# A fused attention and two-layer feed-forward kernel: V of one window pair and the scores of the next as one group in the same two PSUM banks, and pooled attention by two head pairs on the four corners of the array

## The chip, the cores and the metric

The kernel runs on one core of one Trainium2 chip. The metric is the device time of one execution in microseconds. The core has a matrix engine (TensorE, PE in the profile), a vector engine (VectorE, DVE), a scalar engine (ScalarE, ACT), a general engine (GpSimd, POOL) and SyncE (SP), which issues all DMAs of this kernel on one queue. PEld is the loading of weights into the array of TensorE. Every engine works through its own queue in order.

## The reference

`q`, `k`, `v` have the shape (4, 8, 576, 64): batch, heads, positions, head width. Two attentions are added, and the sum runs through two feed-forward layers.

```python
q_d, k_d, v_d = mean of 4 neighbouring positions each        # 144 positions
out_d = softmax(scale * q_d @ k_d.T) @ v_d                   # pooled attention
out_up = np.repeat(out_d, 4, axis=2)
mask = np.abs(pos[:, None] - pos[None, :]) < 4
out_local = softmax(where(mask, scale * q @ k.T, -1e9)) @ v  # band of 7 positions
x = out_up + out_local                                       # as 2304 tokens x 512
x = square(relu(x @ w_in1)) @ w_out1                         # layer one, 512 -> 2048 -> 512
h = x @ w_in2
out = (h * cos(h)) @ w_out2                                  # layer two
```

## The kernel before

The 2304 tokens are cut into 40 windows (10 per batch) of 56 to 60 queries against 64 keys for the band attention. Two neighbouring windows are a pair; there are 20 pairs. Five blocks of four pairs (460 or 464 tokens) go through layer one; layer two follows in nine blocks of 256 tokens.

Layer one is 80 units (5 blocks of 16). A unit has 12 matmuls of stage A (`stage_a`, L801, into the one bank `ps_h`) and 12 of stage B (`stage_b1`, L884, into the four banks `acc`), in a split of each fp32 number into two rounded parts (xh and xl, gh and gl, hi and lo). These 24 are called main matmuls below. Between A and B of a unit, ScalarE makes relu (L825), square (L826) and the high part (L813), and VectorE the low part (L819).

The attention of blocks one to four, and the conversion of the weights (`conv1`, `conv2`), run as tasks beside the units: Python generators that issue a step each time `advance` is called, in the order of `RANK`, from start slots set at the end of the program (`start_at`). The first block's attention runs alone, ahead of all units, in the "early" phase. A scheduler then orders the instructions of each engine by a simulated time line, so attention matmuls end up in groups between main matmuls.

A pair (`pair`, `soft`) on TensorE is: for the first blocks, the mask as a small bf16 matmul (L545); 16 score matmuls of 64 x 64 (L564), each in one corner of the 128 x 128 array (`svs[a][halves_of[c], ...]`: row half a, column half c), into two banks; after the softmax two transposes (L503) per half; and 16 V matmuls (L606), again in corners, into two banks `avs` that are asked for anew. VectorE adds the pooled part (L623), ScalarE and VectorE write xh and xl (L635, L637). PSUM has three banks `ps_a` for all of this.

The pooled attention of a batch is `pool` (loads and sums over four positions, L368, L373, L375; L371 copies the two halves of q into a zero-padded tile `qp`, so that one matmul covers two heads) and four tasks `down`, one for each head pair: three score matmuls with 96 columns of weights over 128 rows (L412), softmax, six transposes of 96 rows (L433), four V matmuls of 64 columns and 72 rows (L449).

The matmuls of `pair` and `down` have plain fp32 operands; each of them is two records in the trace. The transposes and the main matmuls are one record each.

Of the kernel before, what the change touches and what calls it, by code (L numbers as in the profile page):

```python
# [8 lines left out]
F32 = mybir.dt.float32  # L9
# [9 lines left out]
P = 128  # L19
# [11 lines left out]
QROWS = 2 * SD // 3  # L31
DM = H * D
# [16 lines left out]
PE_POOLED = 0  # L49
# [15 lines left out]
RANK = {"down": 0, "pair": 1, "pool": 2, "conv1": 3, "conv2": 3}  # L65
# [27 lines left out]
def kernel(  # L93
# [37 lines left out]
    for t, v in zip(magic, (MAGIC, -MAGIC)):  # L131
# [10 lines left out]
        "a": 3, "h": 1, "acc": 4, "qkw": 2, "vw": 2, "pr": 4, "pt": 5, "xt": 2, "qp": 1, "xd": 2, "vp": 1, "av": 3, "pl": 2, "raw": 2,  # L142
        "dpr": 2, "dpt": 1, "qk0": 0,
# [36 lines left out]
    kept = [spare.pop() for _ in range(W0[1] // 4 + 1)]  # L180
# [28 lines left out]
    lent = {"pr": ["pr"] * caps["pr"] + ['gt', 'gt', 'gl', 'gl'], "pt": ["pt"] * caps["pt"] + ['gh', 'gh', 'gh']}  # L209

    def band_tile(name, shape):
# [5 lines left out]
        if tag == name:  # L217
            return tag, cm.tile(shape, F32, tag=name, name=name, bufs=caps[name])
        t = gp.tile([P, TMAX], F32R if tag in ("gh", "gl") else F32, tag=tag, name=name, bufs=3 if tag == "gh" else 2)
        n = shape[1] * shape[2]  # L220
        return tag, t.bitcast(F32)[:shape[0], :n].rearrange("p (a b) -> p a b", a=shape[1])

    def band_done(name, tag):
        if early[0]:
            lent[name].append(tag)
# [18 lines left out]
    qp = cm.tile([P, HPAIR, 2, SD], F32, name="qp", bufs=1)  # L244
    for a in range(2):
        nc.gpsimd.memset(qp[(1 - a) * D:(2 - a) * D, :, a], 0.0)
    def pool(b):
# [8 lines left out]
        for i, hp in parts:  # L256
# [20 lines left out]
            if b < PE_POOLED:  # L277
                if not early[0]:
                    yield
                bank, = yield from need_a()  # L280
                pe_pool(bank, loaded, kp, vp)
                done_a(bank)
                done("pl")
                done("pl")
                loaded = []
# [48 lines left out]
    def pe_pool(bank, pieces, kp, vp):  # L334
        c0 = 0
        for i, hp, t in pieces:
            if isinstance(i, int):
                rows, cols = P, SD
                tv = t.rearrange("p (j r) -> p r j", r=FACTOR)
            else:  # L340
                rows, cols = KTOK, len(i) * P
                tv = t.rearrange("p (c r) -> p r c", r=FACTOR)
            o = bank[:rows, c0:c0 + cols]
            c0 += cols
            for r in range(FACTOR):
                last["pe"] = nc.tensor.matmul(
                    o, ident[:rows, :rows], tv[:, r], start=r == 0, stop=r == FACTOR - 1
                ).ins
            if i == 0:
                for a in range(2):  # L350
                    half = slice(a * D, (a + 1) * D)
                    nc.scalar.copy(out=qp[half, hp, a], in_=o[half])
            elif i == 1:
                nc.vector.tensor_copy(out=kp[:, hp], in_=o)
            else:
                nc.vector.tensor_copy(
                    out=vp[:, i[0]:i[-1] + 1, hp * P:(hp + 1) * P], in_=o.rearrange("p (k c) -> p k c", k=len(i))
                )

# [4 lines left out]
    def pool_piece(i, hp, t, kp, vp):  # L364
        tv = t.rearrange("p (j r) -> p j r", r=FACTOR)
        if i == 0:
            qc = cm.tile([P, SD], F32, tag="qc", name="qc", bufs=1)
# [33 lines left out]
    def down(b, hp):  # L401
# [8 lines left out]
        qf = qp[:, hp].rearrange("p a s -> p (a s)")  # L410
        for m in range(3):
            last["pe"] = nc.tensor.matmul(sv[:, m], qf[:, m * QROWS:(m + 1) * QROWS], kp[:, hp], start=True, stop=True).ins  # L412
# [5 lines left out]
        yield from exps(s, sv, mx, pr, SCALE / FACTOR ** 2, b < 2)  # L418
# [8 lines left out]
        if not early[0]:  # L427
            yield
# [853 lines left out]
```

## Time and profile before

| what | value |
|---|---|
| median of three runs | 916.42 us (915.8 to 916.44) |
| the profiled execution's own time | 915.9 us |
| its span, first to last instruction | 914.1 us |
| TensorE busy | 891.4 us (98%) |
| VectorE busy | 645.6 us (71%) |
| ScalarE busy | 573.0 us (63%) |
| mean granted TensorE clock | 0.990 of full speed |

The span is what the views of the trace cover; 1.8 us of the execution lie around it. Layer one's first main matmul starts at about 43 us, layer two's first at about 517 us, among the last of layer one. A busy TensorE in such a table is not a TensorE at its peak: how far two starts lie apart tells more than how long one matmul lasts.

### The profile page before, as it was taken

To read this page: it belongs to the slowest core of one execution; us is meant where nothing else is said; L and a number is where in the kernel's file an instruction comes from. 1 tells how busy PE (TensorE), PEld (TensorE's weight loads), DVE (VectorE), ACT (ScalarE), POOL (GpSimd) and SP (SyncE) were. 2 spreads that over 40 slices of the span, in tenths; PEclk is the share of its full clock that TensorE was granted. 3 is DMA by queue.
4 is the path that set the end of the run, shared out by engine and by line. 5 is a ranking of instruction groups with operands and counts; after the bars stand their busy time and mean duration, and the time that the engine had idled before them with its cause. 6 is when DMAs were issued, how large, how long until landed. Compare 5 with 4: busy or idle time off the path is not lost.

```text
span 914.1 us, 17776 instructions
## 1 busy us (share of the span) xinstructions
PE 891.4 (98%) x6946; PEld 814.0 (89%) x6946; DVE 645.6 (71%) x1266; ACT 573.0 (63%) x1039; POOL 97.7 (11%) x79
## 2 busy tenths in 40 slices
PE   7799999999999999999999999999999999999997
PEld 5577788888887888889998999999999999999997
DVE  6999897555766657563311188888888887888786
ACT  5677785455645555454534477776777677777774
POOL 2001320122303313221200000000000000000000
PEclk9799999999999999999999999999999999999999
DMA  9588888867898766884897966655666656566663
GB/s 279 185 324 306 285 305 286 285 254 256 300 331 282 266 231 213 310 307 172 287 386 239 355 222 204 203 187 191 203 202 200 200 200 196 190 196 205 209 227 104
DMA packets 72903, 223.55 MB, mean 245 GB/s; under 512 B 9620, under 2 KB 14612, under 8 KB 68724
## 3 DMA queue, kind: packets, MB, share of 16 engines
q1 hardware_dynamic: 72820, 222.43, 71.5%
q8 instruction: 54, 0.88, 0.4%
q14 instruction: 29, 0.24, 0.1%
HBM read 181.50 MB, written 40.89 MB: 243 GB/s over the span
## 4 chain that ended last, share of the span: by engine, by line
PE 84%; DMA 9%; DVE 3%; ACT 2%; SPq 1%; issue 1%; POOL 0%; DVEq 0%; ACTq 0%; POOLq 0%
PE ps_h L836 22%; PE acc L908 19%; PE ps_h L801 19%; PE acc L884 18%; DMA pl<-in_pool_qk_dram 3%; DMA pl<-in_pool_v_dram 3%; DMA raw<-in_w_dram 2%; DMA pv<-in_pool_v_dram 1%; PE ps_a L412 1%; PE ps_a L606 1%; PE ps_a L564 1%; PE ps_a L449 1%; PE acc L906 1%; PE ps_a L503 1%; PE ps_a L433 1%
## 5 line engine op out<-in xcount | busy, mean ns | idle before, releaser
L836 PE MATMUL ps_h<-x,w2hi 128*128 128x256 f32 x1152 | 160.1, 281 | 0.0
L819 DVE TENSOR_TENSOR gl<-gt,gh 128x460 fp32r<-128x460 f32 (+1 forms) x80 | 59.0, 738 | 141.1 <-ACT gh L813 79.5
L836 PEld LDWEIGHTS ps_h<-x,w2hi 128*128 128x128 f32 x1152 | 146.9, 188 | 0.1
L908 PE MATMUL acc<-bl,gh 128*128 128x256 f32 x504 | 140.6, 280 | 0.0
L801 PE MATMUL ps_h<-xh,w1hi 128*128 128x460 f32 (+1 forms) x320 | 123.3, 386 | 7.4 <-ACT gt L825 3.7
L884 PE MATMUL acc<-gl,w1hi 128*128 128x460 f32 (+1 forms) x320 | 120.5, 377 | 0.2 <-DVE gl L819 0.2
L801 PE MATMUL ps_h<-xl,w1hi 128*128 128x460 f32 (+1 forms) x320 | 120.5, 377 | 0.0
L825 ACT ACTIVATE gt<-ps_h 128x460 f32<-128x460 f32 (+1 forms) x80 | 44.2, 554 | 104.3 <-PE ps_h L801 104.1
L884 PE MATMUL acc<-gh,w1hi 128*128 128x460 f32 (+1 forms) x320 | 107.2, 376 | 0.0
L884 PE MATMUL acc<-gh,lo 128*128 128x460 f32 (+1 forms) x256 | 95.3, 372 | 0.0
L908 PEld LDWEIGHTS acc<-bl,gh 128*128 128x128 f32 x504 | 94.8, 188 | 0.0
L876 DVE TENSOR_TENSOR gl<-g,gh 128x896 fp32r<-128x896 f32 x72 | 78.2, 1087 | 11.0 <-ACT gh L871 11.0
L844 ACT ACTIVATE u<-ps_h,quarter 128x512 f32<-128x512 f32 x72 | 49.4, 687 | 52.6 <-PE ps_h L836 52.4
L908 PE MATMUL acc<-w2hi,gh 128*128 128x256 f32 x288 | 80.7, 280 | 0.0
L908 PE MATMUL acc<-w2hi,gl 128*128 128x256 f32 x288 | 80.2, 280 | 0.0
L851 DVE SCALAR_TENSOR_TENSOR r<-u,ps_h 128x512 f32<-128x512 f32 x72 | 49.4, 687 | 41.3 <-ACT u L846 40.5
L801 PEld LDWEIGHTS ps_h<-xh,w1hi 128*128 128x128 f32 x320 | 60.7, 190 | 17.1 <-ACT gt L825 5.1
L871 ACT ACTIVATE gh<-g 128x896 fp32r<-128x896 f32 x72 | 68.1, 945 | 10.2 <-DVE g L869 10.2
L856 ACT ACTIVATE r<-r,half_pi 128x512 f32<-128x512 f32 x72 | 51.8, 720 | 34.7 <-DVE r L852 34.7
L836 PE MATMUL ps_h<-x,w2lo 128*128 128x256 f32 x432 | 68.5, 280 | 0.0
L884 PEld LDWEIGHTS acc<-gl,w1hi 128*128 128x128 f32 x320 | 60.1, 188 | 7.6 <-DVE gl L819 1.2
L801 PEld LDWEIGHTS ps_h<-xl,w1hi 128*128 128x128 f32 x320 | 60.8, 190 | 6.2
(147 smaller groups left out, 1903.0 us busy)
## 6 DMA issues: line engine op xcount, KB each, us to landing
bl<-wo_d SPq DMA_DIRECT2D x70, 896.0 KB
raw<-in_w_dram SPq DMA_DIRECT2D x32, 1024.0 KB
lo<-lo_d SPq DMA_DIRECT2D x128, 256.0 KB
qkw<-in_win_qk_dram SPq DMA_DIRECT2D x16, 512.0 KB
pl<-in_pool_qk_dram SPq DMA_DIRECT2D x24, 288.0 KB
wo_d<-raw SPq DMA_DIRECT2D x16, 384.0 KB
out_dram<-o SPq DMA_DIRECT2D x18, 256.0 KB
vw<-in_win_v_dram SPq DMA_DIRECT2D x16, 256.0 KB
```

The costliest lines, as they stand in the source:

```text
L412: last["pe"] = nc.tensor.matmul(sv[:, m], qf[:, m * QROWS:(m + 1) * QROWS], kp[:, hp], start=True, stop=True).ins
L801: nc.tensor.matmul(h[:, :n], a[:, c * P:(c + 1) * P], x[:, c, :n], start=i == 0, stop=i == len(order) - 1)
L819: last["gl"] = nc.vector.tensor_tensor(out=gl, in0=gt, in1=gh.bitcast(F32), op=ALU.subtract).ins
L825: last["relu"] = nc.scalar.activation(out=gt, in_=h, func=AF.Relu).ins
L836: nc.tensor.matmul(h[:, s * TB:(s + 1) * TB], a[:, c * P:(c + 1) * P], x[:, c], start=i == 0, stop=i == len(order) - 1,)
L844: nc.scalar.activation(out=u, in_=h, func=AF.Identity, bias=quarter, scale=float(1.0 / (2 * math.pi)))
L851: nc.vector.scalar_tensor_tensor(out=r, in0=u, scalar=-PI2_HI, in1=hv, op0=ALU.mult, op1=ALU.add)
L856: nc.scalar.activation(out=r, in_=r, func=AF.Sin, bias=half_pi, scale=1.0)
L871: nc.scalar.activation(out=gh, in_=g[:, 1:], func=AF.Copy)
L876: nc.vector.tensor_tensor(out=gl, in0=g[:, 1:], in1=gh.bitcast(F32), op=ALU.subtract)
L884: nc.tensor.matmul(acc[d][:, :n], a, x, start=f == 0 and i == 0, stop=f == NF - 1 and i == 2)
L908: nc.tensor.matmul(o, a[:, x], b, start=opens and i == 0, stop=p == NP2 - 1 and i == 2 and (k % 2 == 1 or k == NPROD - 1),)
```

## The change

- `down` serves batch 0 alone. For batches 1 to 3 a task `down_two` serves two head pairs at once. Its scores are 12 matmuls of 64 x 64 weights over 144 columns, one head each, in the four corners (row half a: head of the pair; column half c: head pair). The queries are taken in three parts of 48; the weights have 64 columns, so 16 rows of each part hold what is not used. The transposes are then of 128 rows in place of 96. The V matmuls stay, eight in one go.
- `qp` needs no zero padding for these, so the sum over positions writes q directly, without the copies L371. The tile is lengthened by a strip of zeros.
- In `pair`, the score matmuls are now a function. When V of a pair is issued and the next pair waits with its scores, these are issued right behind, into the upper halves of the same two banks (V uses 256 columns of 512). A pair waits for that unless it is `alone`; V is held back a little for a next pair that is about to come (`held_for_next`).
- One buffer fewer for `pt`, one more for `dpt`; the unused `pe_pool` is gone.

```diff
-RANK = {"down": 0, "pair": 1, "pool": 2, "conv1": 3, "conv2": 3}
+RANK = {"down": 0, "down_two": 0, "pair": 1, "pool": 2, "conv1": 3, "conv2": 3}
...
-        "a": 3, "h": 1, "acc": 4, "qkw": 2, "vw": 2, "pr": 4, "pt": 5, "xt": 2, "qp": 1, "xd": 2, "vp": 1, "av": 3, "pl": 2, "raw": 2,
-        "dpr": 2, "dpt": 1, "qk0": 0,
+        "a": 3, "h": 1, "acc": 4, "qkw": 2, "vw": 2, "pr": 4, "pt": 4, "xt": 2, "qp": 1, "xd": 2, "vp": 1, "av": 3, "pl": 2, "raw": 2,
+        "dpr": 2, "dpt": 2, "qk0": 0,
...
-            if t is not None:
+            if t is not None and shares.pop(id(t), 1) == 1:
                 used[kinds.pop(id(t))[0]] -= 1
...
-        if i == 0:
-            qc = cm.tile([P, SD], F32, tag="qc", name="qc", bufs=1)
+        if i == 0 and not early[0]:
+            nc.vector.tensor_reduce(out=qp[:, hp, 0], in_=tv, op=ALU.add, axis=AX.X)
+        elif i == 0:
+            qc = cm.tile([P, HPAIR * 2 * WQ], F32, tag="xt", name="qc", bufs=caps["xt"])[:, :SD]
...
+    def down_soft(b, a, s, sv, pr, pts):
...
+        for kt in range(2):
+            for m in range(3):
+                last["pe"] = nc.tensor.transpose(
+                    tps[kt][:KTOK, m * P:(m + 1) * P], pr[:, m, kt * KTOK:(kt + 1) * KTOK], ident,
+                ).ins
...
+    def down_two(b, h2):
...
+        ss = yield from need_a(2)
+        svs = [s[:, :3 * SD].rearrange("r (m s) -> r m s", m=3) for s in ss]
+        halves_of = [slice(a * D, (a + 1) * D) for a in range(2)]
+        for m in range(3):
+            for c in range(2):
+                q0 = 2 * (2 * h2 + c) * SD + m * QPART
+                for a in (1, 0):
+                    rows = halves_of[a]
+                    with in_turn(m + c > 0 or a == 0):
+                        last["pe"] = nc.tensor.matmul(
+                            svs[a][halves_of[c], m], qf[rows, q0:q0 + D], kp[rows, 2 * h2 + c], start=True, stop=True,
+                        ).ins
...
+    def alone(q):
+        if q - 1 < W0[1] // 2 or placed[0] >= q or q - 1 not in scored_pairs:
+            return True
+        b = window_of(2 * q - 2)[0]
+        return any((b, hp) not in downs for hp in range(HPAIR))
+
+    def held_for_next(q, j):
+        if q + 1 == NW // 2 or q + 1 in scored_pairs or q + 1 in at_scores:
+            return False
+        return now[0] < NF * j - 3 and begins[q + 1] < now[0] + 5
...
+        if ss is None:
+            ss = yield from need_a(2)
+            svs = [s[:, :HPAIR * WK].rearrange("p (h s) -> p h s", h=HPAIR) for s in ss]
+            scores(svs)
+        else:
+            svs = [s[:, 4 * WQ:].rearrange("p (h s) -> p h s", h=HPAIR) for s in ss]
...
+        while not apart and held_for_next(q, j):
+            yield
         avs = yield from need_a(2)
...
+        if q + 1 in at_scores and q + 1 not in handed:
+            at_scores[q + 1](
+                [t[:, 4 * WQ:].rearrange("p (h s) -> p h s", h=HPAIR) for t in avs], follows=True
+            )
+            handed[q + 1] = avs
+            for t in avs:
+                shares[id(t)] = 2
...
-        for hp in range(HPAIR):
-            start_at(at + 4 + hp, down, b, hp)
+        for h2 in range(HPAIR // 2):
+            start_at(at + 4 + 2 * h2, down_two, b, h2)
```

What this does to the queue of TensorE is shown at two places. Line numbers of the change are its own: L890 and L973 are the main matmuls of stages A and B, L632 the scores and L691 the V matmuls of a pair, L484 and L453 scores and transposes of `down_two`, L559 the transposes of a pair.

TensorE before, in block four's attention (units 50 and 51): the V matmuls of pair 17 and one score matmul of pair 18 stand together, and the other 15 scores after 26 further main matmuls.

```order
L884 MATMUL acc_4560<-gh,lo 128x460
L606 MATMUL ps_a<-pt,vw 64x56 x14
L564 MATMUL ps_a<-qkw 64x64
L801 MATMUL ps_h_4603<-xh,w1hi_800 128x460
L801 MATMUL ps_h_4603<-xl,w1hi_800 128x460
```

The rest of these scores, with main matmuls on both sides:

```order
L884 MATMUL acc_4557<-gh,lo 128x460
L884 MATMUL acc_4558<-gh,w1hi_685 128x460
L564 MATMUL ps_a<-qkw 64x64 x15
L801 MATMUL ps_h_4643<-xh,w1hi_805 128x460
L801 MATMUL ps_h_4643<-xl,w1hi_805 128x460
```

TensorE with the change, the same V matmuls, now in unit 52:

```order
L973 MATMUL acc_4519<-gl,w1hi_795 128x460
L973 MATMUL acc_4519<-gh,lo 128x460
L691 MATMUL ps_a<-pt,vw 64x56 x16
L632 MATMUL ps_a<-qkw 64x64 x16
L890 MATMUL ps_h_4686<-xh,w1hi_910 128x460
L890 MATMUL ps_h_4686<-xl,w1hi_910 128x460
```

V and scores are one group of 32 matmuls where they were three groups. Eight of the 16 pairs behind the early phase are joined so.

TensorE before, pooled scores of batch 3 (unit 42): three matmuls for one head pair, then transposes of a window pair and pooled V.

```order
L884 MATMUL acc_3455<-gl,w1hi_1289 128x464
L884 MATMUL acc_3455<-gh,lo 128x464
L412 MATMUL ps_a<-kp,qp 96x144 x3
L503 MATMUL ps_a<-const_sb,pr 128x128 x2
L449 MATMUL ps_a<-dpt,vp 64x144 x4
L801 MATMUL ps_h_4085<-xh,w1hi_1524 128x464
```

TensorE with the change, pooled scores of batch 3 (unit 42): twelve matmuls for two head pairs.

```order
L973 MATMUL acc_3410<-gh,lo 128x464
L973 MATMUL acc_3411<-gh,w1hi_1271 128x464
L484 MATMUL ps_a<-kp,qp 64x144 x12
L559 MATMUL ps_a<-const_sb,pr 128x128 x2
L890 MATMUL ps_h_4062<-xh,w1hi_1515 128x464
L890 MATMUL ps_h_4062<-xl,w1hi_1515 128x464
```

Six such groups of twelve take the place of twelve groups of three; in four of the six the first matmul stands by itself, some main matmuls ahead of the other eleven.

ScalarE before, from the high part of unit 36 to the relu of unit 37 (gt, L825): an exponential (L397) stands ahead of the relu.

```order
L813 ACTIVATE gh<-gt 128x464
L684 ACTIVATE shi<-bits 128x1024
L397 ACTIVATE pr<-pr 128x256
L825 ACTIVATE gt<-ps_h_3544 128x464
L771 ACTIVATE raw<-raw 128x768
L397 ACTIVATE pr<-pr 128x256
```

ScalarE with the change, the same stretch (L914 is the relu, L915 the square, L902 the high part, L727 xh, L370 the exponential):

```order
L902 ACTIVATE gh<-gt 128x464
L773 ACTIVATE shi<-bits 128x1024
L727 ACTIVATE xh<-xt 128x4x116
L914 ACTIVATE gt<-ps_h_3492 128x464
L860 ACTIVATE raw<-raw 128x768
L915 ACTIVATE gt<-gt 128x464
L370 ACTIVATE pr<-pr 128x256
```

What stands ahead of this relu is now a copy of the sum of both attentions (xh), and the exponentials come later.

## Rows read from the trace of the kernel before

**Rows 1.** The page, busy time of the engines, and the chain that ended last.
```profile
PE 891.4 (98%) x6946; PEld 814.0 (89%) x6946; DVE 645.6 (71%) x1266; ACT 573.0 (63%) x1039; POOL 97.7 (11%) x79
...
PE 84%; DMA 9%; DVE 3%; ACT 2%; SPq 1%; issue 1%; POOL 0%; DVEq 0%; ACTq 0%; POOLq 0%
```

**Rows 2.** Busy time by stretch: length, engines (instructions), granted clock, DMA share, GB/s.
```profile
75.00:100.00 25.00, 23.24 (x153) 19.83 (x152) 22.99 (x47) 18.51 (x52) 3.74 (x3) 0.93 0.84 294
125.00:150.00 25.00, 25.00 (x214) 20.93 (x213) 21.91 (x45) 17.81 (x35) 1.64 (x2) 1.00 0.88 287
275.00:300.00 25.00, 23.00 (x167) 19.11 (x166) 15.26 (x33) 13.62 (x23) 8.07 (x5) 1.00 0.88 292
550.00:914.00 364.00, 359.11 (x3012) 357.57 (x3011) 302.95 (x561) 257.34 (x363) 0.00 (x0) 1.00 0.59 195
```

**Rows 3.** Waits of TensorE, whole span: us in total, times, longest.
```profile
PE ps_h L801 <- ACT gt L825: 3.7, 3, 2.0
...
PE ps_h L801 <- ACT w1hi L684: 1.8, 1, 1.8
PE ps_a L503 <- POOL pr L491: 1.4, 1, 1.4
```

**Rows 4.** Time line of TensorE, V matmuls: start, duration, engine, line, tile, records.
```profile
234.41 0.37 PE L884 MATMUL acc<-gh,w1hi 128*128 128x460 f32 x1
234.71 0.33 PE L606 MATMUL ps_a<-pt,vw 64*64 64x60 f32 x4
...
235.28 0.37 PE L884 MATMUL acc<-gh,lo 128*128 128x460 f32 x1
235.58 0.69 PE L606 MATMUL ps_a<-pt,vw 64*64 64x60 f32 x32
...
236.52 0.38 PE L801 MATMUL ps_h<-xl,w1hi 128*128 128x460 f32 x1
```

**Rows 5.** Time line of TensorE, pooled scores of one head pair alone.
```profile
193.73 0.37 PE L884 MATMUL acc<-gh,lo 128*128 128x460 f32 x1
193.93 0.90 PE L412 MATMUL ps_a<-kp,qp 128*96 128x144 f32 x6
194.57 0.47 PE L801 MATMUL ps_h<-xh,w1hi 128*128 128x460 f32 x1
194.88 0.38 PE L801 MATMUL ps_h<-xl,w1hi 128*128 128x460 f32 x1
195.09 0.37 PE L801 MATMUL ps_h<-xh,w1hi 128*128 128x460 f32 x1
```

**Rows 6.** Time line of TensorE, pooled transposes ahead of pooled scores.
```profile
211.19 0.66 PE L433 MATMUL ps_a<-const_sb,dpr 96*72 96x96 f32 x6
211.69 0.90 PE L412 MATMUL ps_a<-kp,qp 128*96 128x144 f32 x6
```

**Rows 7.** Time line of TensorE, scores of a pair and pooled V in one group.
```profile
228.85 0.69 PE L564 MATMUL ps_a<-qkw 64*64 64x64 f32 x32
229.48 0.71 PE L449 MATMUL ps_a<-dpt,vp 72*64 72x144 f32 x8
230.12 0.48 PE L801 MATMUL ps_h<-xh,w1hi 128*128 128x460 f32 x1
```

**Rows 8.** Time lines of VectorE and then ScalarE, 278 to 282 us.
```profile
278.80 0.68 DVE L375 TENSOR_REDUCE vp<-pl 72x128 f32<-72x512 f32 x1 [1.11 <-DMA pl<-in_pool_v_dram]
279.40 0.87 DVE L480 TENSOR_TENSOR pr<-ps_a,const_sb 128x128 f32<-128x128 f32 x4
...
281.29 0.42 ACT L397 ACTIVATE pr<-pr 128x256 f32<-128x256 f32 x1 [4.91 <-DVE pr L393]
281.62 0.54 ACT L825 ACTIVATE gt<-ps_h 128x464 f32<-128x464 f32 x1
```

**Rows 9.** Groups by line: additions and copies; records, busy, mean ns, idle before.
```profile
L623 DVE TENSOR_TENSOR xt<-ps_a,xd 128x232 f32<-128x232 f32 (+1 forms) x32 | 11.1, 387 | 2.7 <-PE ps_a L606 2.5
...
L371 ACT COPY qp<-qc 64x144 f32<-64x144 f32 x32 | 9.9, 310 | 14.4 <-DVE qc L368 14.0
```

More of the change, by code (lines that the diff above doesn't have):

```diff
@@ L31 @@
 QROWS = 2 * SD // 3
+QPART = SD // 3
 DM = H * D
@@ L179 @@
     spare = list(range(AHEAD, NF))
-    kept = [spare.pop() for _ in range(W0[1] // 4 + 1)]
+    kept = [spare.pop() for _ in range(W0[1] // 4 + 2)]
     held, taken = {}, {}
@@ L276, in pool @@
                     yield
[L277 to L285, printed above, removed]
             while loaded:
@@ L332, in early_v @@
         bands["vp"] = vp
[L334 to L348, printed above, removed]
-            if i == 0:
[L350 to L358, printed above, removed]
     def pool_sum(*piece):
@@ L409, in down @@
         sv = s[:QROWS, :3 * SD].rearrange("r (m s) -> r m s", m=3)
[L410 removed]
+        qh = qp[:, hp].rearrange("p a s -> p (a s)")
         for m in range(3):
[L412 removed]
+            last["pe"] = nc.tensor.matmul(sv[:, m], qh[:, m * QROWS:(m + 1) * QROWS], kp[:, hp], start=True, stop=True).ins
         qk_used[b] = qk_used.get(b, 0) + 1
@@ new lines, in down_two @@
+    def down_two(b, h2):
+        while b not in pooled:
+            yield
+        _, kp, vp = pooled[b]
+        if b not in xds:
+            xds[b] = cm.tile([P, HPAIR, SD], F32, tag="xd", name="xd")
+        yield from need("dpr", 2)
+        prs = []
+        for a in range(2):
+            prs.append(task_tile("dpr", P, 3 * SD).rearrange("p (m s) -> p m s", m=3))
+        ss = yield from need_a(2)
[10 more added lines that the diff above has]
+                        ).ins
+        qk_used[b] = qk_used.get(b, 0) + 1
+        if qk_used[b] == HPAIR // 2:
+            done("qp")
+        pts = [None, None]
+        runs = [down_soft(b, a, ss[a], svs[a], prs[a], pts) for a in range(2)]
+        second = [runs.pop(1)]
+        while runs or second:
+            for r in list(runs):
+                if next(r, "end") == "end":
+                    runs.remove(r)
+            runs += second
+            second = []
+            yield
+        av, = yield from need_a()
+        avv = av[:, :2 * SD].rearrange("p (c s) -> p c s", c=2)
+        for c in range(2):
+            for kt in range(2):
+                for a, rows in enumerate(halves_of):
+                    v0 = (2 * h2 + c) * P + a * D
+                    last["pe"] = nc.tensor.matmul(
+                        avv[rows, c], vp[:, kt, v0:v0 + D], pts[a][:, kt, c], start=kt == 0, stop=kt == 1,
+                    ).ins
+        done("dpt", 2)
+        vp_used[b] = vp_used.get(b, 0) + 1
+        if vp_used[b] == HPAIR // 2:
+            done("vp")
+        nc.scalar.copy(out=xds[b][:, 2 * h2:2 * h2 + 2], in_=avv)
+        done_a(av)
+        downs.update((b, 2 * h2 + c) for c in range(2))
@@ new lines, in pair @@
+        ss = None
+        if not apart:
+            at_scores[q] = scores
+            while q not in handed and not alone(q):
+                yield
+            del at_scores[q]
+            ss = handed.pop(q, None)
+        if ss is None:
+            ss = yield from need_a(2)
+            svs = [s[:, :HPAIR * WK].rearrange("p (h s) -> p h s", h=HPAIR) for s in ss]
+            scores(svs)
+        else:
+            svs = [s[:, 4 * WQ:].rearrange("p (h s) -> p h s", h=HPAIR) for s in ss]
@@ L656, in behind @@
         return nullcontext()
-    def in_turn(follows):
-        return tc.issue_after(last["pe"]) if follows and not early[0] else nullcontext()
     def split(raw, hi, los=None, sums=None, held_back=None):
```

112 lines of the change are left out of this document (69 added, 43 removed).

## The prediction

> **What bounds the kernel now.** I read the page first. TensorE is busy for 891.4 of 914.1 us, and 84% of the chain that ended last is TensorE's [rows 1]. Such a share is a mean over stages, so the stretches come next. From 125 to 150 us, and over all of layer two, TensorE has work in every microsecond or nearly so: 25.00 of 25, 359.11 of 364. VectorE is close behind in the first stage alone (22.99 of 25 between 75 and 100 us) [rows 2]. The waits of TensorE are then few: 3.7 us for relu results, of which one is 2.0 us, 1.8 us for converted weights, 1.4 us for GpSimd [rows 3]. So in layer one the time is the length of TensorE's queue, and an attention matmul costs what it adds to that queue. The busy column doesn't tell that, since matmuls overlap; the starts on the time line do.
>
> **Prices.** Two main matmuls in a row start 0.21 us apart (194.88 and 195.09) [rows 5]. The price of a group of attention matmuls is therefore the time from the start of the last main matmul ahead of it to the start of the second one behind it, less 0.42 us. The first start behind a group alone won't do, since that matmul too is slower to follow (0.31 us).
>
> - Three pooled scores, six records, alone: 194.88 - 193.73 - 0.42 = 0.73 us. The records take (194.57 - 193.93) / 6 = 0.107 us each, and 0.09 us is the price of being a group [rows 5].
> - V matmuls in corners: four records cost 235.28 - 234.41 - 0.42 = 0.45 us, 32 cost 236.52 - 235.28 - 0.42 = 0.82 us. The difference, 0.37 us over 28 records, is 0.0132 us a record of 60 columns; what is left, 0.40 us, is the price of a group in corners whatever its size [rows 4].
> - Pooled transposes: (211.69 - 211.19) / 6 = 0.083 us each at 96 columns [rows 6].
>
> So a corner matmul is cheap, and coming into the corners and out of them is dear: 0.40 against 0.09 us for a group that uses the whole array. The Trainium skill has a rule for that (TensorEngine Tiling (Array Packing), Key Properties): changing the tiling mode drains TensorE. That speaks against the pooled half of this change, which takes scores from the whole array into corners. The trace agrees with the direction, by the 0.31 us between the two prices [rows 4, 5]; if the rule cost nothing here, the third term below would be -0.5 in place of -1.8.
>
> **The change part by part.**
>
> *Pooled scores.* Twelve groups of six records go: 72 x 0.107 = 7.7 us. Six groups of 24 records come, 144 records of 144 columns. No row shows this form. The nearest row has the same corners in the same rotation, with fewer columns [rows 4]: 0.0132 x 144 / 60 = 0.032 us, 4.6 us in all. The other end is the pooled V record, as many columns in two halves of the array: (230.12 - 229.48) / 8 = 0.080 us [rows 7], 11.5 us in all. I take 0.032, since scores of a pair in corners, 32 records in 229.48 - 228.85 = 0.63 us [rows 7], follow the price of V too. Term: -3.1 us, with +3.8 us as the other end.
>
> *Pooled transposes.* As many, but of 128 columns in place of 96. By columns 72 x 0.083 x (128 / 96 - 1) = +2.0 us; the other end is 0, if the start of each is what counts. I take +2.0.
>
> *Groups.* Counted over the order of TensorE from the third main unit on, 53 groups with corner matmuls and 25 without become 49 and 23. Eight joins of V and scores take groups away; four of the six pooled score groups give some back, as their first matmul stands by itself and pays the 0.40 us again. Term: 4 x 0.40 + 2 x 0.09 = -1.8 us. Number and kind of the pairs' matmuls stay. If only the two groups without corners were to count it would be -0.2, if each of the eight joins kept its full 0.40 it would be -3.2.
>
> *The wait of 2.0 us.* TensorE's longest wait is for the relu at 281.62 us. ScalarE held it behind an exponential that waited 4.91 us for VectorE, where a pooled sum waited for its load until 278.80 and the masks, maxima and differences followed [rows 8]. In the changed order a copy to xh stands there, and on VectorE only the addition L623 is between it and the two late sums. Two additions of 0.39 us [rows 9] after the sum that ends at 279.48 let xh start near 280.3, and if xh takes as long as the relu behind it (0.54 us [rows 8]), the relu starts near 280.8: 0.8 us sooner. The ends are -2.0 (the load comes earlier against TensorE) and +2.0 (it comes as much later). I take -0.8.
>
> *ScalarE.* The 24 copies L371 of batches 1 to 3 go: 24 x 0.31 = 7.4 us [rows 9]. ScalarE is busy 63% of the span [rows 1] and on the chain for 2%, so I cost that at nothing; its cover is TensorE's own queue. VectorE keeps the number and free sizes of its operations: as many sums, maxima and exponential sums, over 128 rows in place of 96, which run side by side. GpSimd multiplies the same 432 columns twelve times.
>
> *The early phase and layer two.* The queues are the same up to the first unit, and in layer two. Nothing.
>
> *Buffers and waits.* V may be held back for the next pair's scores, which waits with V itself; behind a held V on TensorE stand main matmuls, but the hold is in the order, not a semaphore, so others go first. What a join adds is that both banks stay taken from V until the next pair's maxima, and one bank of the three is left for all transposes. In the order V still ends 0.8 to 1.3 units ahead of the block that needs it, as before. I take nothing here; the price of such a wait is in the rivals.
>
> Sum: -3.1 + 2.0 - 1.8 - 0.8 = -3.7 us. The profiled execution took 915.9 us, 1.8 us beyond its span and 0.5 us under the median of the runs. It would take 912.2; against the median of 916.4 that is 912.7 us.
>
> **Rivals.**
>
> *More than the sum: the early waits go as well.* The wait for converted weights (1.8 us [rows 3]) falls into 75 to 100 us, and the granted clock there is 0.93, so some of that stretch ran at 1.2 GHz after TensorE stood still: 25 x 0.07 = 1.75 us lost [rows 2]. If ScalarE, without its copies, delivers earlier, both go, and with them the remaining 1.2 us of the relu wait: 912.7 - 4.75 = 908.0 us. For it: ScalarE is busy 18.5 of 25 us there. Against it: VectorE is the fuller one, and it keeps its work.
>
> *The corners don't run together at 144 columns.* Then each record costs as a pooled V record, 0.080 us, and the first term is +3.8: 912.7 + 6.9 = 919.6 us, slower than before. The gain is gone from 0.057 us a record on. For it: pooled V, also 144 columns, keeps to 0.080 with two halves. Against it: the two rows with four corners, and that pooled V has 72 rows, more than half of the array, and so only its column halves to share.
>
> *Banks run short.* With two of three banks held through a join, a transpose waits for a bank, at the head of TensorE's queue with all main matmuls behind it. Its price is the 1.4 us of the one transpose that waited [rows 3]. There are eight joins and six pooled groups, which also hold two banks; three such waits give 912.7 + 4.2 = 916.9, no change, and five 919.7. For it: the transposes of a pair, users of these banks, stand in the list already. Against it: the order was made with the same three banks, and the shares of waiting in layer one are small.
>
> **How the numbers follow.** My sum 0.62, the early waits go too 0.17, corners not together 0.09, banks short 0.12. The likeliest case has its own range of 910.2 to 914.9 us (transposes between 0 and +2.0, the group term between -0.2 and -3.2, not all at one end). A measurement of this kernel can tell 0.2% from no change, 1.8 us: faster is below 914.6, slower above 918.2. Faster: 0.57 of the first case, 0.17 of the second and 0.02 of the others, 0.76. Same: 0.05 of the first, 0.06 of the banks and 0.04 of the corners, 0.15. Slower: 0.09. The range that should hold the time 8 times in 10 reaches down to the case of the early waits and up to where three bank waits eat the gain: 908.0 to 916.9 us.
>
> **What would show it.** In the profile after: pooled scores of 24 records start to next main matmul in 0.76 + 0.21 us, about 1.0, if corners run together, over 1.9 if not. A joined group of 64 records costs 0.40 + 64 x 0.0132 = 1.24 us against 1.64 for two. Transposes of six take 0.66 us where they took 0.50. Layer one's last main matmul comes about 3.7 us earlier and layer two takes as long as before. TensorE's waits list shows no wait of 2 us for relu and no new rows for transposes or scores. I am wrong if the list of waits grows by over 4 us, or if the starts in layer two move apart.

## The result, and the profile after

The changed kernel is slower: 923.06 us as the median of four runs (921.91 to 923.64) against 916.42 (915.8 to 916.44), ratio 1.0068 with a 95% interval of 1.0049 to 1.0086. The forecast was 912.7. On another chip, beside 17 runs of the kernel before, it was 923.57 against 916.22, ratio 1.0081 [1.0056, 1.0107]. So the loss is 6.6 to 7.4 us and it repeats.

The page of the profiled execution (span 921.0 us, its own time 922.82) answers [rows 1]; columns as there.

```profile
PE 891.8 (97%) x7018; PEld 814.1 (88%) x7018; DVE 643.5 (70%) x1266; ACT 565.0 (61%) x1009; POOL 99.5 (11%) x80
```

TensorE is as busy as before, ScalarE has lost 8.0 us of work, and the span is 6.9 us longer. What has grown is TensorE's standing still. The busy time by stretch (length, engines, granted clock, DMA share, GB/s) answers [rows 2], with the stretch from 100 to 125 us added:

```profile
75.00:100.00 25.00, 23.40 (x184) 19.16 (x182) 22.80 (x48) 19.42 (x57) 6.92 (x6) 1.00 0.94 315
100.00:125.00 25.00, 20.45 (x142) 16.92 (x139) 23.06 (x42) 19.14 (x51) 5.64 (x5) 0.96 0.89 300
125.00:150.00 25.00, 25.00 (x212) 20.59 (x212) 20.02 (x38) 14.29 (x26) 2.00 (x2) 0.98 0.74 247
275.00:300.00 25.00, 24.14 (x193) 20.07 (x192) 16.50 (x37) 12.23 (x22) 9.31 (x5) 1.00 0.90 310
```

From 75 to 100 us it got better: the clock is 1.00 where it was 0.93. From 275 to 300 too: the wait of 2.0 us for the relu is gone. From 100 to 125 us TensorE is idle for 4.55 us; before, it was busy for 23.33 of these 25 us. The waits of TensorE from 45 to 525 us (us in total, times, longest) say for whom:

```profile
PE ps_h L890 <- ACT gt L914: 5.0, 4, 2.2
PE ps_a L453 <- ACT pr L359: 3.1, 1, 3.1
PE ps_a L559 <- POOL pr L547: 2.1, 1, 2.1
...
PE acc L973 <- ACT y L1011: 1.2, 1, 1.2
PE acc L973 <- ACT gh L902: 0.8, 1, 0.8
PE acc L973 <- DVE gl L908: 0.8, 1, 0.8
PE ps_a L613 <- ACT pr L359: 0.6, 1, 0.6
```

In [rows 3] the list was 3.7, 1.8 and 1.4 us and little else. New are the pooled transposes (L453), which waited 3.1 us for exponentials of a pair (L359) to leave a bank. The transposes of a pair (L559) waited for GpSimd before too (L503, 1.4 us); they wait longer now, and the rows under them are new or were under 0.3 us. The row left out is the first unit's wait for xh, 1.9 us, which took 1.8 us before (at 43.5 us).

The first main matmul of each unit on the time line shows where the time is lost ("again" and "moved" are two of the experiments below: the same kernel once more, and with one conversion moved).

| start of, in us | before | after | again (e11) | moved (e12) |
|---|---|---|---|---|
| unit 0 | 43.5 | 44.8 | 44.2 | 43.4 |
| unit 10 | 112.8 | 111.6 | 110.1 | 110.3 |
| unit 16 | 152.8 | 159.5 | 157.9 | 155.8 |
| unit 32 | 248.7 | 257.5 | 255.4 | 253.0 |
| unit 48 | 352.6 | 358.8 | 356.6 | 354.2 |
| unit 79 | 512.5 | 519.4 | 517.7 | 514.9 |
| layer two | 517.5 | 524.4 | 522.7 | 520.0 |

At unit 10 the changed kernel is ahead by 1.2 us, at unit 16 behind by 6.7. These six units took 47.9 us in both of its profiles, and 40.0 before; of these 7.9 us, 1.7 are eight more main matmuls that now fall into them, 5.4 are standing still and half clock, and 0.8 are attention. Later stretches add 2.2, give back 2.6 and add 0.7. Layer two is the same.

### The profile page after: what moved, and what is told of

It is laid out like the page before. It is cut to its first block, busy times and chain, and to the rows that moved or that the text cites. A ratio compares the mean times of both kernels' runs of the same rounds, so it can differ in the third digit from the quotient of the medians.

```text
span 921.0 us, 17894 instructions
## 1 busy us (share of the span) xinstructions
PE 891.8 (97%) x7018; PEld 814.1 (88%) x7018; DVE 643.5 (70%) x1266; ACT 565.0 (61%) x1009; POOL 99.5 (11%) x80
## 4 chain that ended last, share of the span: by engine, by line
PE 59%; DMA 1%; DVE 0%; ACT 0%; DVEq 0%; issue 0%; ACTq 0%
PE ps_h L925 22%; PE acc L997 19%; PE acc L973 9%; PE ps_h L890 8%; PE acc L995 1%; DMA wo_d<-raw 1%; PE ps_a L691 0%; PE ps_a L559 0%; PE ps_a L632 0%; DVE o L1035 0%; DVE st L1035 0%; ACT y L1011 0%; DVEq L1368 0%; ACTq L1011 0%
## 5 line engine op out<-in xcount | busy, mean ns | idle before, releaser
L908 DVE TENSOR_TENSOR gl<-gt,gh 128x460 fp32r<-128x460 f32 (+1 forms) x80 | 55.9, 699 | 146.6 <-ACT gh L902 88.1
L890 PE MATMUL ps_h<-xh,w1hi 128*128 128x460 f32 (+1 forms) x320 | 123.0, 385 | 7.7 <-ACT gt L914 5.0
L973 PE MATMUL acc<-gl,w1hi 128*128 128x460 f32 (+1 forms) x320 | 120.6, 377 | 0.8 <-DVE gl L908 0.8
L890 PE MATMUL ps_h<-xl,w1hi 128*128 128x460 f32 (+1 forms) x320 | 120.6, 377 | 0.0
L914 ACT ACTIVATE gt<-ps_h 128x460 f32<-128x460 f32 (+1 forms) x80 | 44.2, 553 | 119.4 <-PE ps_h L890 119.2
L973 PE MATMUL acc<-gh,w1hi 128*128 128x460 f32 (+1 forms) x320 | 101.2, 375 | 2.0 <-ACT y L1011 1.2
L973 PE MATMUL acc<-gh,lo 128*128 128x460 f32 (+1 forms) x256 | 95.4, 373 | 0.0
L890 PEld LDWEIGHTS ps_h<-xh,w1hi 128*128 128x128 f32 x320 | 60.7, 190 | 17.3 <-ACT gt L914 7.0
L960 ACT ACTIVATE gh<-g 128x896 fp32r<-128x896 f32 x72 | 68.1, 946 | 10.6 <-DVE g L958 10.6
L973 PEld LDWEIGHTS acc<-gh,w1hi 128*128 128x128 f32 x320 | 59.5, 188 | 9.7 <-ACT y L1011 1.6
L973 PEld LDWEIGHTS acc<-gl,w1hi 128*128 128x128 f32 x320 | 60.1, 188 | 8.2 <-DVE gl L908 1.1
```

The source lines that it names most:

```text
L890: nc.tensor.matmul(h[:, :n], a[:, c * P:(c + 1) * P], x[:, c, :n], start=i == 0, stop=i == len(order) - 1)
L908: last["gl"] = nc.vector.tensor_tensor(out=gl, in0=gt, in1=gh.bitcast(F32), op=ALU.subtract).ins
L914: last["relu"] = nc.scalar.activation(out=gt, in_=h, func=AF.Relu).ins
L960: nc.scalar.activation(out=gh, in_=g[:, 1:], func=AF.Copy)
L973: nc.tensor.matmul(acc[d][:, :n], a, x, start=f == 0 and i == 0, stop=f == NF - 1 and i == 2)
```

## What stood at 118 us

ScalarE's time line of the changed kernel (start, duration, engine, line, operation, tile; in brackets the idle time ahead and what ended it):

```profile
113.89 1.17 ACT L755 ACTIVATE bits<-raw 128x1024 f32<-128x1024 f32 x1
118.29 1.15 ACT L755 ACTIVATE bits<-raw 128x1024 f32<-128x1024 f32 x1 [3.23 <-DMA raw<-in_w_dram]
119.32 0.32 ACT L359 ACTIVATE pr<-ps_a,mx 128x64 f32<-128x64 f32 x1
...
121.34 0.34 ACT L359 ACTIVATE pr<-ps_a,mx 128x64 f32<-128x64 f32 x1
121.63 0.59 ACT L914 ACTIVATE gt<-ps_h 128x460 f32<-128x460 f32 x1
122.06 0.43 ACT L459 COPY dpt<-ps_a 72x288 f32<-72x288 f32 x1
```

Two conversions of weights stand in a row. The second (of weight tile 13, the fourteenth; tiles count from 0) needs a tile that is still on its way, and ScalarE stands for 3.23 us. Behind it in the queue are the eight exponentials of a pair, which free the two banks with scores, then a relu, then the copy that frees the third bank. TensorE's time line of the same moments:

```profile
117.02 0.37 PE L973 MATMUL acc<-gl,w1hi 128*128 128x460 f32 x1
117.23 0.37 PE L973 MATMUL acc<-gh,lob 128*128 128x460 f32 x1
120.66 0.52 PE L453 MATMUL ps_a<-const_sb,dpr 128*72 128x128 f32 x3 [3.06 <-ACT pr L359]
121.83 0.30 PE L613 MATMUL ps_a<-const_b 64*64 64x256 bf16 x2 [0.65 <-ACT pr L359]
...
122.80 0.55 PE L890 MATMUL ps_h<-xh,w1hi 128*128 128x460 f32 x1
123.15 0.59 PE L890 MATMUL ps_h<-xl,w1hi 128*128 128x460 f32 x1
123.53 0.59 PE L890 MATMUL ps_h<-xh,w1hi 128*128 128x460 f32 x1
```

The transposes stand at the head of TensorE's queue with all main matmuls behind them, and soon after TensorE runs again the main matmuls take 0.59 us and start 0.38 us apart (123.15 and 123.53), not 0.21: the granted clock is at 1.2 GHz for 3.4 us from 122.8 on. In the kernel before, the same conversion waited for its tile too, 1.44 us, until a later moment of the program:

```profile
115.41 0.30 ACT L386 ACTIVATE pr<-ps_a,mx 128x64 f32<-128x64 f32 x1
...
118.02 0.56 ACT L825 ACTIVATE gt<-ps_h 128x460 f32<-128x460 f32 x1
120.02 1.13 ACT L666 ACTIVATE bits<-raw 128x1024 f32<-128x1024 f32 x1 [1.44 <-DMA raw<-in_w_dram]
```

There the exponentials and the relu were ahead of it. The tile did not come later after the change (118.29 against 120.02); the operation that waits for it moved ahead of the exponentials. The Trainium skill has the rule in PSUM — Partial Sum Buffer, section "Engine vs sequencer instructions": the queues of ScalarE, VectorE and GpSimd are strict FIFO. This trace agrees: VectorE had the scores' maxima ready at 117.02 us, and the exponentials ran only behind the conversion, from 119.32 on.

```profile
116.79 0.23 DVE L356 TENSOR_SCALAR mx<-mx 128x4 f32<-128x4 f32 x2
```

So about 2.3 of the 3.06 us are the conversion's doing.

Theory A is therefore: the loss is the place of that conversion in ScalarE's queue. Rivals: B, the pooled work on corners costs more than its records show; C, the joins cost it.

## The experiments

Each was timed beside runs of the kernel before on the same chip. Their medians are 917.06 (e1 to e4), 917.09 (e5 to e7), 917.03 (e8 to e10) and 916.22 us (e11, e12).

**e1, the pooled half alone: no joined groups.**

```diff
+JOIN_FROM = 99
-        if q - 1 < W0[1] // 2 or placed[0] >= q or q - 1 not in scored_pairs:
+        if q < JOIN_FROM or q - 1 < W0[1] // 2 or placed[0] >= q or q - 1 not in scored_pairs:
...
-        if q + 1 == NW // 2 or q + 1 in scored_pairs or q + 1 in at_scores:
+        if q + 1 < JOIN_FROM or q + 1 == NW // 2 or q + 1 in scored_pairs or q + 1 in at_scores:
```

> Pooled attention by two head pairs as in the change, no pair's scores joined to another's V. Theory A (the loss is in units 0 to 16, where the new order puts exponentials behind a weight load that is late, so that transposes wait for their bank, and moves attention past the units in which TensorE waits for weights anyway): its order up to unit 12 is again another, so the waits there are drawn anew; 914 to 920 us, and the sum of TensorE's waits decides which. Theory B (the corner scores are what costs): as slow as the whole change, 921 to 924 us. Theory C (the joins are what costs, by the banks that they hold): 913 to 915 us, faster than before.

923.91 us (921.67 to 927.76), ratio 1.0070 [1.0044, 1.0096]. The pooled half alone loses as much as the whole. That is the range of theory B; theory A's 914 to 920 us was missed. ScalarE in this kernel, near the same place in the program, and then TensorE:

```profile
118.17 1.18 ACT L756 ACTIVATE bits<-raw 128x1024 f32<-128x1024 f32 x1 [0.19 <-DMA raw<-in_w_dram]
...
123.73 1.12 ACT L756 ACTIVATE bits<-raw 128x1024 f32<-128x1024 f32 x1 [4.11 <-DMA raw<-in_w_dram]
124.75 0.55 ACT L915 ACTIVATE gt<-ps_h 128x460 f32<-128x460 f32 x1
```

```profile
125.35 0.47 PE L891 MATMUL ps_h<-xh,w1hi 128*128 128x460 f32 x1 [2.83 <-ACT gt L915]
```

Again a conversion holds ScalarE's queue, but it is the next one, of weight tile 14; tile 13's ran at 118.17 with a wait of 0.19 us. A relu is caught behind it, not a bank, so a bank is not needed for such a wait. But this wait is not most of e1's loss: unit 16 starts 1.7 us later than before (154.6 us), unit 79 8.3 us later (520.8). Nor is it the clock, whose mean over the timed runs is 0.9898 (0.9888 in the runs of before). B is not settled by this run.

**e2, the joins alone: pooled attention by head pairs, as before.**

```diff
+TWO_FROM = 9
...
-        for h2 in range(HPAIR // 2):
+        for h2 in range(HPAIR // 2 if b >= TWO_FROM else 0):
             start_at(at + 4 + 2 * h2, down_two, b, h2)
+        for hp in range(HPAIR if b < TWO_FROM else 0):
+            start_at(at + 4 + hp, down, b, hp)
```

The edit also puts back the buffers and the steps of `down` that the change had altered (not shown).

> V and scores joined as in the change, pooled attention by one head pair as before, buffers as before. Theory A: as in the pooled half, units 0 to 16 decide, 914 to 921 us. Theory B: faster than before by what the joins save, 912 to 915 us. Theory C: 920 to 924 us. If the 1.3 us that the whole change loses ahead of the first unit come from where its tiles lie, the first main matmul starts at 43.5 us here, as before, and not at 44.8.

918.30 us (916.49 to 922.09), ratio 1.0018 [0.9999, 1.0036]. The joins by themselves cost next to nothing, and bring nothing. C falls.

**e3, the change from the second block of attention on:** the edits of e1 and e2 with `JOIN_FROM = 8` and `TWO_FROM = 2`, so that the first pooled batch runs as before. The buffers of `pt` and `dpt` are the change's here; the strip of zeros is gone and `mx` has seven buffers for eight.

> Joins from pair 8 on alone, and batch 1 pooled by one head pair as before; the order of TensorE is that of before up to unit 12. Theory A: unit 16 starts within 1.5 us of the kernel before, and what is left is the shorter queue behind unit 16 (about 2 us) less the new waits there (2 to 3 us): 913 to 917 us. Theory B: pooled scores in corners for two of three batches, so some 4 of the 6.6 us of loss stay: 919 to 922 us. Theory C: all joins but the first are here, so 920 us and more.

916.63 us (914.59 to 920.12), ratio 0.9999 [0.9980, 1.0019]. With the stretch around 118 us in its old order, the rest of the change is free of loss, as theory A expected.

**e4, the whole change, with one conversion moved by one step.**

```diff
+        for _ in range(1 if f == 13 else 0):
+            yield
         hi1[f] = wp.tile([P, 2 * DM], F32R, tag=f"hi{f}", name=f"w1hi{f}")
```

> The whole change, with the conversion of the fourteenth weight tile held back by one step, so that ScalarE does a pair's eight exponentials ahead of it; the order of TensorE is that of the change up to unit 12. Theory A: the wait of 3.06 us of the pooled transposes goes down to under 1 us, the half clock behind it (1.7 us lost) may go too, and unit 13 starts 2 to 4 us earlier: 918 to 921 us. Theories B and C: this load is not the cause, another wait takes its place at once, 922 to 924 us.

917.11 us (914.46 to 918.95), ratio 0.9997 [0.9982, 1.0011]. All of the change is in it, and by the medians the loss is gone, a little further than theory A's 918 to 921 us. ScalarE, and then TensorE:

```profile
115.57 0.32 ACT L359 ACTIVATE pr<-ps_a,mx 128x64 f32<-128x64 f32 x1 [2.00 <-DVE mx L356]
...
120.82 1.18 ACT L755 ACTIVATE bits<-raw 128x1024 f32<-128x1024 f32 x1
```

```profile
116.91 0.52 PE L453 MATMUL ps_a<-const_sb,dpr 128*72 128x128 f32 x3 [0.77 <-ACT pr L359]
```

The conversion runs at 120.82 without waiting, the exponentials at 115.57, and the transposes' wait is 0.77 us in place of 3.06. In units 10 to 16 TensorE stands still for 1.7 us in place of 4.0; the half clock stays (3.4 us from 119.3 on). The profiled execution's span is 4.5 us shorter, and units 10 to 16 give 2.4 us of it; 1.6 lie ahead of unit 0 and 1.2 in units 16 to 32, where the move was not aimed. B falls as the cause of the whole change's loss: its corner matmuls are all still there.

**e5, the same move in the kernel before** (nothing of the change).

> The kernel before, with nothing of the change, and the conversion of weight tile 13 one step later. Theory A (the changed kernel lost because ScalarE's operation on a late weight stood ahead of what TensorE needed): in the kernel before that operation waited 1.44 us for its transfer at 120.0 us, and TensorE waited there for nothing that the profile shows over 1 us, so there is little to win: ratio to before 0.998 to 1.002 (915 to 919 us). Rival D (moving that conversion is a gain of its own, which any version of the kernel would take, and says nothing of the change): some 6 us less, ratio 0.992 to 0.995.

920.29 us (917.12 to 922.03), ratio 1.0036 [1.0008, 1.0064]. The move is no gain of its own, which rules D out. It even costs, more than theory A allowed: a new wait of 2.11 us stands at 173.2 us, for the addition to xt.

**e6, the same move in e1's kernel.**

> Pooled attention by two head pairs on corners, no joined groups, and the conversion of weight tile 13 one step later. In the version without the move ScalarE's operation on a weight waited 4.11 us for its transfer at 123.7 us, a relu stood behind it, and TensorE waited 2.83 us for the relu, with 3.4 us at the half clock behind that. Theory A: that wait goes, and with it 2.83 us and about 1.7 us of half clock: 923.9 - 4.5 = 919.4 us, 918 to 921. Rival B (the pooled work on corners costs more than its records show): the wait goes or moves, the time stays at 922 to 925 us.

926.07 us (922.63 to 930.95), ratio 1.0109 [1.0068, 1.0151]. Theory A's number was missed by 6.7 us, and rival B's 922 to 925 us is nearer: the wait did not go, it grew. ScalarE, and then TensorE:

```profile
125.09 1.12 ACT L756 ACTIVATE bits<-raw 128x1024 f32<-128x1024 f32 x1 [5.20 <-DMA raw<-in_w_dram]
```

```profile
126.71 0.75 PE L893 MATMUL ps_h<-xh,w1hi 128*128 128x460 f32 x1 [4.03 <-ACT gt L917]
```

The wait is the one of e1 (ScalarE stands 5.20 us, TensorE 4.03 behind it, 6.8 us at 1.2 GHz follow). But it is again the conversion of tile 14, and the edit moved that of tile 13, which waited 0.19 us in e1 and runs without a wait here, at 118.41 us. So e6 did not move the operation that held ScalarE, and theory A is not tested by it. The profiled execution was the longest of the four (930.95 us; the others took 922.63 to 927.92).

**e7, the whole change, the move, and layer two's conversions one unit earlier** (`17 + int(3 * u)` for `18 + int(3 * u)` in the start slots of `conv2`).

> The whole change, the conversion of weight tile 13 one step later, and every conversion of layer two's weights one unit earlier. The waits left after unit 16 in the version with the conversion of tile 13 moved alone are 0.93 (182.6 us), 0.76 (285.9), 1.74 (362.4) and 1.31 us (366.5), the last behind a copy on ScalarE that waited 2.31 us until a converted weight had left its buffer. Theory A carried on (the order of ScalarE's queue around weights decides the rest too): the last three go, 917.1 - 3.8 = 913.3 us, 912 to 915. Rival E (such waits come up elsewhere when one set of them is moved, as many as before): 916 to 919 us, with other waits of 1 to 2 us after unit 16.

919.11 us (915.88 to 920.81), ratio 1.0023 [1.0003, 1.0042]. The waits at 286 to 367 us went, from unit 32 to 79 it took 257.7 us (263.8 before), but a wait of 3.73 us came at 187.6 us, behind a pooled sum on VectorE that waited for its load. Rival E was right here.

**e8, e9, e10: that shift from the fifth conversion on** (`(17 if u >= 4 else 18) + int(3 * u)`), in e3's kernel, in e4's kernel and in the kernel before.

> Units 0 to 16 as before the change (the first pooled batch by head pairs, joined groups only from pair 8 on), the change from there on, and layer two's conversions from the fifth on one unit earlier. From unit 32 to 79 the version with all of these conversions earlier took 257.7 us, before 263.8; from unit 0 to 32 before took 205.2 us, the late version without this shift 208.3, of which 3.3 us is half clock. Theory A (waits of ScalarE's and VectorE's queues on transfers decide, and they are set by where the conversions fall): the short late part comes over, 916.6 - 5.7 = 911 us, 909 to 913. Rival E (waits come up as often wherever the conversions fall): 915 to 919 us.

> The whole change, the conversion of weight tile 13 one step later, and layer two's conversions from the fifth on one unit earlier. Theory A: the wait of 3.73 us at 187.6 us, which came with the earlier start of the first four, is gone, and units 32 to 79 stay at 257.7 us instead of 262.4: 917.1 - 4.7 = 912.4 us, 910 to 914. Rival E: 915 to 919 us.

> The kernel before with layer two's conversions from the fifth on one unit earlier, nothing of the change. Its one wait of over 0.2 us after unit 16 was 2.00 us at 282.2. Theory A: at most that wait can go and no wait is bound to come, so 914 to 918 us, ratio 0.997 to 1.001. Rival F (the earlier conversions are worth some 5 us to any version): 910 to 912 us, ratio 0.993 to 0.995.

916.16 us (914.0 to 922.1), ratio 0.9993 [0.9973, 1.0014]; 915.65 us (911.79 to 921.2), ratio 0.9988 [0.9966, 1.0010]; 916.42 us (913.54 to 920.46), ratio 0.9990 [0.9972, 1.0008]. None can be told from the kernel before, and rivals E (915 to 919 us) and, in e10, theory A (914 to 918) held; F did not. Theory A's 911 and 912.4 us were missed by 3 to 5 us, though in e9 no single wait of TensorE from 45 to 525 us is over 1.2 us (the longest rows of its list):

```profile
PE ps_h L892 <- ACT gt L916: 4.5, 6, 1.1
PE ps_h L892 <- ACT w1hi L773: 1.1, 2, 0.8
PE ps_a L453 <- ACT pr L359: 0.8, 1, 0.8
```

e9's profiled execution took 913.84 us, near its expectation; its other runs spread over 9 us. It is the fastest version by its median, and no proof that the change can win: e10, the kernel before with the same shift, has 916.42 us, and its profiled execution took 913.54.

**e11 and e12, the whole change and e4's kernel again, side by side.**

> The whole change once more, beside the same with one conversion moved, on one chip. Theory A (ScalarE's queue behind the late weight tile at 118 us): slower than before by 4 to 7 us again, with the wait of some 3 us at 120 us. Whether the first unit begins at 44.8 us again (after 17.1 us at the half clock) or at 43.3 us (after 10.2 us) is open; if it is 43.3, that part of the loss, 1.3 to 1.5 us, was the run's and not the change's. Rival G (the first chip's difference was its own): within 0.2% of before.

> The whole change with the conversion of weight tile 13 one step later, on the same chip as the whole change again. Theory A: 4 to 6.6 us under the whole change beside it, and within 0.2% of before. Rival G: no difference between the two.

923.57 us (921.07 to 925.42), ratio 1.0081 [1.0056, 1.0107], and 918.11 us (915.96 to 922.03), ratio 1.0024 [1.0008, 1.0040]. The move gives back 5.5 of 7.35 us; the two intervals are apart. The loss is a little above theory A's 4 to 7 us, and e12 stays 0.24% above before, just outside its 0.2%. TensorE in e11 and then in e12:

```profile
118.36 0.86 PE L453 MATMUL ps_a<-const_sb,dpr 128*72 128x128 f32 x3 [2.25 <-ACT pr L359]
```

```profile
117.10 0.52 PE L453 MATMUL ps_a<-const_sb,dpr 128*72 128x128 f32 x3 [0.78 <-ACT pr L359]
```

The wait explains only part of the 5.5 us. Units 10 to 16 took 47.9 against 45.5 us, 2.4 us, as between the first profile of the change and e4. Another part is the clock. Over all timed runs the mean granted clock was 0.9850 in e11 and 0.9893 in e12 (0.9862 in the first runs of the change, 0.9900 in e4, 0.9888 to 0.9895 in the runs of before beside e4 and e12); 0.0043 of 917 us is 3.9 us of full speed. From run to run of one kernel the time rises by 0.4 to 0.75 us for each such us (a line through the runs of e11, e12, e4 and e9), which makes 1.6 to 2.9 us. In the profile some of it follows the wait (6.8 us from 118.3 on), some lies ahead of unit 0, where e11 has 13.7 us and the first profile 17.1, against 10.2 in before and in e12. TensorE's order there is the same in all of these, and e4, e7, e9 and e12, which hold the whole change too, had 10.2 us, while e3 and e5 had 17.1 and 13.7. So it does not go with the change; what sets it stays open, and so does the share of the 5.5 us that neither the wait nor the clock covers.

## Why the prediction was wrong, step by step

I add up TensorE's time from unit 0 to 79 by parts: standing still (gaps of over 50 ns), loss to the half clock (half of its length), main matmuls (0.2075 us each), and what is left, the attention.

| us | before | after | e11 | e12 | e4 | e9 | e1 | e6 | e2 | e3 |
|---|---|---|---|---|---|---|---|---|---|---|
| standing still | 7.5 | 14.6 | 12.6 | 10.9 | 13.1 | 8.8 | 15.3 | 16.0 | 11.1 | 8.7 |
| half clock | 3.4 | 3.4 | 5.1 | 3.4 | 1.7 | 1.7 | 1.7 | 8.5 | 3.4 | 6.7 |
| attention | 69.7 | 68.1 | 67.3 | 68.8 | 68.4 | 68.3 | 72.2 | 71.7 | 69.5 | 67.9 |

The first two rows together, by units:

| us | 0 to 10 | 10 to 16 | 16 to 32 | 32 to 48 | 48 to 79 |
|---|---|---|---|---|---|
| before | 8.4 | 0.3 | 0.0 | 2.2 | 0.0 |
| after | 6.4 | 5.7 | 2.1 | 0.9 | 2.9 |
| e11 | 5.6 | 6.2 | 1.7 | 0.8 | 3.4 |
| e12 | 6.0 | 3.4 | 1.0 | 0.8 | 3.0 |
| e4 | 6.2 | 3.4 | 0.9 | 1.2 | 3.1 |
| e1 | 5.4 | 4.5 | 2.7 | 2.9 | 1.5 |

*The step that failed: "Buffers and waits ... I take nothing here."* Standing still grew by 7.1 us (5.1 in e11); this term alone turns the sum, and it is over the 4 us that the prediction itself named as the sign of being wrong. The prediction looked for the wait of a transpose for a bank, in a rival, and priced it at 1.4 us with a chance of 0.12; it came once, at 3.06 us (2.25 in e11), and not because two banks are held through a join (the scores in them were issued at 110.40 us, with no V beside them), but because the exponentials that free them stood behind a conversion that waited for its weights. Two more of the new waits are of the same kind: 2.14 us at 175.9, where GpSimd's product waited for a reciprocal behind two pooled sums on VectorE, and these for their load,

```profile
173.39 1.38 DVE L348 TENSOR_REDUCE vp<-pl 72x128 f32<-72x512 f32 x2 [2.96 <-DMA pl<-in_pool_v_dram]
174.70 0.16 DVE L546 RECIPROCAL mx<-mx 128x4 f32<-128x4 f32 x1
```

and 1.2 us at 371, where the copies of y waited for a store to free their buffer:

```profile
370.45 0.99 ACT L1011 COPY y<-acc 128x464 f32<-128x464 f32 x2 [2.19 <-DMA wo_d<-raw]
```

A wait of 1.73 us at 367.1 is of another kind: the relu stood behind a copy to xh that waited 1.01 us for an addition on VectorE, and no transfer stands in it.

*"ScalarE ... I cost that at nothing."* The copies of [rows 9] went, ScalarE is busy 8.0 us less (7.4 were worked out), and that brings nothing. But the argument, busy 63% and 2% of the chain, says nothing about an in-order queue in which one operation waits for a transfer: from 45 to 130 us ScalarE's waits for weight tiles went from 4.6 to 9.8 us (6.1 in e11).

*The wait of 2.0 us at 282 [rows 8].* It went, with 0.76 us for VectorE at 290.6 in its place. Right, and small beside what came.

*Pooled scores.* Right in price. 24 records in corners stand where two groups like that of [rows 5] stood; TensorE's time line:

```profile
98.82 0.36 PE L890 MATMUL ps_h<-xl,w1hi 128*128 128x460 f32 x1
99.11 0.97 PE L484 MATMUL ps_a<-kp,qp 64*64 64x144 f32 x24
100.01 0.44 PE L559 MATMUL ps_a<-const_sb,pr 128*128 128x128 f32 x2
```

From their start to that of the next group it is 0.90 us; the forecast had about 1.0. That is 0.038 us a record, against the 0.080 of the rival. Corners run together at 144 columns, and the rival that they don't is wrong. The saving is small even so, since four of the six groups are split: at 72.9 and 76.8 us the first matmul and the other eleven cost 0.59 and 1.08 us, 1.67 together, by the prediction's way of pricing a group, and two groups like that of [rows 5] cost 1.46.

*Pooled transposes.* TensorE's time line again, for six of them:

```profile
209.32 0.82 PE L453 MATMUL ps_a<-const_sb,dpr 128*72 128x128 f32 x6
209.98 0.38 PE L559 MATMUL ps_a<-const_sb,pr 128*128 128x128 f32 x2
```

They take 0.66 us, as forecast, where the 96 columns of [rows 6] took 0.50.

*Groups.* A joined group of 64 records, against the V matmuls of [rows 4]:

```profile
360.53 1.01 PE L890 MATMUL ps_h<-xh,lo 128*128 128x460 f32 x4
361.46 0.69 PE L691 MATMUL ps_a<-pt,vw 64*64 64x58 f32 x32
361.97 0.65 PE L632 MATMUL ps_a<-qkw 64*64 64x64 f32 x32
362.56 0.48 PE L890 MATMUL ps_h<-xh,w1hi 128*128 128x460 f32 x1
362.87 0.37 PE L890 MATMUL ps_h<-xl,w1hi 128*128 128x460 f32 x1
```

The last of the four main matmuls ahead starts at about 360.53 + 3 x 0.21 = 361.16, so the group costs 362.87 - 361.16 - 0.42 = 1.29 us; 1.24 was forecast. (There are nine joins in the order, not the eight that the text ahead says.) Scores, transposes and groups together were to give -2.9 us; the attention row of the table gives -1.6 and, in e11, -2.4. (The same order gives between 67.3 and 68.8 us in after, e11, e12, e4 and e9, so the row is good to about 1 us.) The joins alone leave the attention as it is (e2). Counting groups on the time lines from unit 0 to 79 says why: those with corner matmuls or pooled V go from 55 to 52, but the others from 26 to 40, -1.2 and +1.3 us at the prediction's prices. The pooled half alone lengthens the attention by 2.5 us (e1; 2.0 in e6). It has 59 and 19 groups where the whole change has 51 and 23, which makes 2.8 of the 4.1 us between the two. Against the kernel before, the prices would have e1 about even. So without the joins rival B is right to some 2 us, and what they are stays open.

*The likeliest case's range.* Its upper end, 914.9 us, does not follow from the two terms named: the transposes stand at their upper end already, and the group term at -0.2 gives 914.3.

*The early phase and layer two: "Nothing".* Layer two is right. Unit 0 began 1.3 and 0.7 us later, after a longer stretch at 1.2 GHz in a phase whose order is unchanged; e4 and e12, with the same phase, began 0.2 and 0.1 us earlier than before, so this does not go with the change.

*The rival "early waits go as well".* They did: up to unit 10 the kernel gained 2.5 us, the wait of 1.8 us for a weight at 89 us is 0.3, and the clock from 75 to 100 us is full. That it was for want of the copies is not shown: e2 keeps them and gained 2.3 us there. And it was not kept: ScalarE's wait for tile 13 was 1.44 us at 120.0 before and 3.23 us at 118.3 now.

So the change shortens TensorE's queue by 0.9 to 2.4 us, where 2.9 were worked out, and what came of it was decided mostly by where a handful of waiting operations fall in the queues of two engines that are idle for 30 and 39% of the span. With the one conversion moved, standing still is 3.4 us above before in e12 and 5.6 in e4 and eats the gain; in e9, with 1.3 us above, the versions are even.

## What to carry to other kernels

Where in-order engines mix work that waits for transfers with work that another engine waits for, list before any change, for each operation that waits for a transfer, what stands behind it; a change that moves the order is worth what it does there before it is worth what it saves in the bounding queue. An engine's low busy share is no cover against this. When a change of a few microseconds loses, move the one waiting operation and nothing else before giving up on the change, and make the same move in the kernel before as a control. Make sure first that it is the operation that waits: in e6 it was its neighbour, and the run decided nothing. And add up the trace after the move, too: here the medians gained 5.5 to 5.9 us, and the stretch that the move was aimed at gave 2.4.

## What was not expected of the hardware

A group of 64 records of fp32 corner matmuls costs nearly as its count says (1.29 us each time, at 278.0, 361.5 and 386.7 us of the changed kernel), so the price of entering and leaving the corners, 0.40 us, is paid once, even when the operands and banks' halves change inside. The half-clock stretch ahead of unit 0 was 10.2 us in before, e1, e2, e4, e6, e7, e9, e10 and e12, 13.7 in e5, e8 and e11, and 17.1 in e3 and the first profile of the change, with unit 0 between 42.8 and 45.0 us accordingly; it moves the whole program by up to 2 us, and it differs between two executions of the same kernel (17.1 and 13.7 us in the whole change). The same kernel spread over 6 to 8 us from run to run on the later chips, where the first chip's four runs of the kernel before lay within 0.7 us.
